# Attention with a mixture-of-experts tail: buffers for the bias groups, the place of the k, q and table loads, and the tiling of the reciprocals

## The chip, the cores and the metric

One NeuronCore of a Trainium2 chip runs the whole kernel. The metric is device time in microseconds (us). The kernel before takes 1065.97 us in the median of three runs (1064.12 to 1066.11).

## The reference, cut to what matters

Attention over 2 batches, 8 heads, 576 positions and 64 dimensions per head, with a position bias that a small network computes from the distance of two positions; two mixture-of-experts layers follow.

```python
scores = scale * np.matmul(q, k.transpose(0, 1, 3, 2))
psi_rel = np.log1p(np.abs(rel)); psi_i = np.log1p(np.maximum(pos[:, None], 1.0))
h = np.maximum((psi_rel / psi_i)[..., None] @ w1 + b1, 0.0)
bias = h @ w2                                   # one plane per head, the same for both batches
scores = scores + bias.transpose(2, 0, 1)[None]
attn = np.exp(scores - max); attn = attn / (sum + 1e-9)
x = attn @ v; x = moe(x); return moe2(x)
```

## The kernel before, in words

**Bias groups.** The 576 rows of the bias are computed in 36 groups of 16 rows, and eight groups make one 128-row chunk of the bias, `nb`. For a group g, `h_pieces` (L511) computes four hidden planes of 576 columns, each one instruction on a window of a table `win` of logarithms: for even groups VectorE (DVE) and ScalarE (ACT) do two each, for odd groups DVE does three and ACT one. `b_pieces` (L525) multiplies them on TensorE (PE) with the output weights into a PSUM bank pair, copies that, scaled by a row's factor, to an SBUF buffer `r` (the "out" of a group: for the first nine groups on DVE if g is even and on ACT if it is odd, afterwards on DVE), and a DMA spreads `r` over the partitions of `nb` (the "row" of a group, 288 KB). Hidden planes have two buffers (`hbs`), `r` has three (`rs2`), and the first nine groups take turns in three PSUM pairs, `pB`, `pT`, `sc`. `sc` is also the pair of the scores.

**Scores.** The first attention tile needs all eight rows of the first chunk. `s_pieces` (L628) multiplies q and k for one head into `sc`; one custom DVE instruction (in the trace `CUSTOM_DVE_ANT_0`) adds the bias from `nb` and finds the extreme; ACT takes the exponential. Transposes (`t_pieces`) and the product with v (`v_pieces`, column tiles of 128x64) follow. There are 9 tiles of 8 heads. `over` (L715) makes reciprocals of the sums and spreads them over partitions by four matmuls with 128x128 weights, twice a tile.

**Loads.** q and k arrive in float32 and are split in two float16 parts. For k (`load_k`, L565, four heads a load, two DMAs of 288 KB) DVE casts and subtracts. For q (`load_q`, L580) ACT casts and, for the first two loads, DVE subtracts. The staging buffers `stg` are two, and the loads take turns in them. k0 (heads 0 to 3 of batch 0), q0, the cast of the identity and k2 (heads 4 to 7) stand ahead of the bias groups in the program; the second part of the table, which only groups from 8 on read, is loaded behind the row of group 2 (`load_table`, ACT scales it). The dictionary `loads` (L620) says behind which group's row each other load is issued. All these DMAs are issued by SP, one queue.

**Order.** The program is recorded and then ordered by a planner (`Plan`, L47): every operation has an assumed cost, a due time counted back from the end and its data dependencies; an engine takes the ready operation that is due first. Marks (`plan.order`) add dependencies that data doesn't give. What the planner fixes is the order on each engine; on the chip each instruction then waits for its own inputs. One plan covers the bias, the attention and the start of the first expert layer. The work behind it is planned separately.

Of the kernel before, what the change touches and what calls it, by code (L numbers as in the profile page):

```python
# [10 lines left out]
F32 = mybir.dt.float32  # L11
# [3 lines left out]
ACTF = mybir.ActivationFunctionType  # L15
# [10 lines left out]
HS = 288  # L26
# [321 lines left out]
def attn_moe_moe_kernel(ctx: ExitStack, tc: tile.TileContext, a, out):  # L348
# [37 lines left out]
    def carve(t, *parts, off=0):  # L386

        out = []
        for shape, dtype in parts:
            out.append(at(t, off, shape, dtype))  # L390
            off += -(-int(np.prod(shape)) * mybir.dt.size(dtype) // 64) * 64
        return out
# [3 lines left out]
    def turn_of(ring):  # L396
        i = turns[id(ring)] = turns.get(id(ring), -1) + 1
        return ring[i % len(ring)]
# [15 lines left out]

    nbv = [at(t, 0, [H, S], F32) for t in nbr]
    hbs = carve(r_bias, *[([4, S], F32)] * 2)
    win, per_row = carve(r_bias, ([ROW0 + S], F32), ([144 + 36], F32), off=18432)
    shift, ipsi = per_row[:, 0:144], per_row[:, 144:]
    rs2 = carve(r_bias, *[([S], F32)] * 2, off=23744) + [at(r_w, 6144, [S], F32)]
# [8 lines left out]
    es2 = carve(r_e, *[([2 * S], F32)] * 3)  # L428
    ets = carve(r_e, *[([9, 128], F32)] * 2, off=13824)
    rbs, xts = (carve(t, *[([2, 128], F32)] * 2, off=o) for t, o in ((r_st, 8192), (r_e, 23040)))  # L430
    stg = [at(r_st, 0, [2, S], F32), at(r_w, 512, [2, S], F32)]
    wpk, sst = carve(r_w, ([2 + H], F32), ([4, H], F32))
    mns = [sml.tile([128, H], F32, name=f"mn{i}") for i in range(2)]
# [24 lines left out]
    pheads = psum_pool("pheads", 1, stack)  # L458
    sc, pT, pB = (pheads.tile([128, 1024], F32, name=n) for n in ("sc", "pT", "pB"))
    pO, pR = (pheads.tile([128, 512], F32, name=n) for n in ("pO", "pR"))  # L460
    pb0, pb = [pB, pT, sc], [pB]

    blk4 = const.tile([128, 4], F32, name="blk4")
    cst, ident16, ones, lg, P, pt, rs, cs, wgs, wg = carve(
# [26 lines left out]
    def warm(ps, n):  # L491
        with plan.together():
            for _ in range(n):
                pe.matmul(out=ps, lhsT=idle[:, 0:128], rhs=idle[:, 0:ps.shape[-1]], start=True, stop=True,
                          skip_group_check=True)

    warm(pO, 9)

    vec.tensor_scalar(shift, shift, b1, None, ALU.mult)
    vec.tensor_scalar(w2r, w2r, C_S, None, ALU.mult)  # L500
# [9 lines left out]

    def h_pieces(g):  # L511

        hb = hidden[g] = turn_of(hbs)

        def piece(u):
            m = ROW0 - rows_of[g][4 * u]
            x, by = win[:, m:m + S], shift[:, 4 * g + u:4 * g + u + 1]
            if u in BY_VECTOR[g % 2]:
                vec.tensor_scalar(hb[:, u], x, by, 0.0, ALU.add, ALU.max)
            else:  # L520
                act.activation(hb[:, u], x, ACTF.Relu, bias=by)

        return [lambda u=u: piece(u) for u in range(4)]

    def b_pieces(g):  # L525

        c, q = groups[g]
        r = turn_of(rs2)
        if q == 0:
            nbs[c] = turn_of(nbv)  # L530

        def piece():
            ps = turn_of(pb0 if g < EARLY else pb).rearrange("p (j n) -> p j n", j=2)[:, :, 0:HS]
            with plan.together():
                for jh in range(2):
                    for u in range(4):
                        pe.matmul(
                            out=ps[32 * u:32 * u + 32, jh], lhsT=sst, rhs=hidden[g][:, u, jh * HS:jh * HS + HS], start=True,
                            stop=True, tile_position=(0, 32 * u), skip_group_check=True,
                        )  # L540
            two = r.rearrange("p (j n) -> p j n", j=2)
            if g < EARLY and g % 2:
                act.activation(two, ps, ACTF.Copy, scale=ipsi[:, g:g + 1])
            else:
                vec.tensor_scalar(two, ps, ipsi[:, g:g + 1], None, ALU.mult)
            nb = nbs[c]
            with plan.order(mark=[("rows", g)]):
                if c < 4:
                    sp.dma_start(out=nb[q::8], in_=r)
                else:  # L550
                    for b in range(B):
                        for p in range(2):
                            sp.dma_start(out=nb[64 * b + q + 4 * p:64 * b + 64:8], in_=r[64 * p:64 * p + 64])
            for load, which in loads.get(g, ()):
                load(which, [("rows", g)])

        return [piece]
# [7 lines left out]
    def load_k(p, behind=()):  # L565

        (b, h), t = divmod(2 * p, H), turn_of(stg).rearrange("p i (j n) -> p (i j) n", j=2)
        for half in range(2):
            me = slice(64 * half, 64 * half + 64)
            load(t[me], a["kT"][me, 2 * p:2 * p + 4, HS * half:HS * half + HS], behind)  # L570
        hi, lo = (x[b][:, h:h + 4] for x in (kh, kl))
        vec.tensor_copy(hi, t)
        tt(vec, lo, t, hi, ALU.subtract)

    for b in range(B):
        for half in range(2):
# [3 lines left out]
    def load_q(t, behind=()):  # L580

        b0, n, c0, w = (t % 2, 1, 128 * (t // 2), 128) if t < 8 else (0, 2, 512, 64)
        x = turn_of(stg).rearrange("p i s -> p (i s)")[:, 0:1024].rearrange("p (h w) -> p h w", w=w)
        load(x, a["qT"][:, H * b0:H * b0 + H * n, c0:c0 + w], behind)
        for b in range(b0, b0 + n):
            xb = x[:, H * (b - b0):H * (b - b0) + H]
            hi = qh[:, 4 * b:4 * b + 4].rearrange("p i j s -> p (i j) s")[:, :, c0:c0 + w]
            act.activation(hi, xb, ACTF.Copy)
            for lo, h in [(qls[0], 0)] if b == 0 else [(qls[1], 0), (qls[2], 4)]:
                n_ = lo.shape[1]  # L590
                tt(vec if t < 2 else pool, lo[:, :, c0:c0 + w], xb[:, h:h + n_], hi[:, h:h + n_], ALU.subtract)

    def load_v(b, behind=()):

# [14 lines left out]
    def load_constants(i, behind=()):  # L609
# [2 lines left out]
        load(cst[:, j], a["cst"][:, j], behind)  # L612

    load_table(0)
    load_k(0)
    load_q(0)
    load_constants(0)
    vec.tensor_copy(ident16, ident)
    load_k(2)
    loads = {  # L620
        2: [(load_table, 1)], 7: [(load_v, 0)], 8: [(load_k, 4), (load_q, 1)], 9: [(load_k, 6)], 10: [(load_v, 1)],
        12: [(load_q, 2)], 13: [(load_q, 3), (load_constants, 1)], 18: [(load_q, 4)], 19: [(load_q, 5)],
        24: [(load_q, 8)], 27: [(load_q, 6)], 28: [(load_q, 7)],
    }
# [90 lines left out]
    def over(t, a_):  # L715

        s = state[t]
        (r, rs_), rb = turn_of(r4s), turn_of(rbs)
        vec.tensor_scalar(r, s["sm"][:, 4 * a_:4 * a_ + 4], 1e-9, 1.0 / C_X, ALU.add, ALU.mult)
        vec.reciprocal(r, r)  # L720
        rw = r.unsqueeze(2).to_broadcast([128, 4, D])
        eng = vec if t in ROW_TILES[-2:] else pool
        eng.tensor_copy(rs_[:, 0], rw)
        tt(eng, rs_[:, 1], rw, rs_[:, 0], ALU.subtract)
        ps = pR[:, 0:256].rearrange("p (k i) -> p k i", k=2)
        with plan.together():
            for k in range(2):
                for i in range(2):
                    pe.matmul(
                        out=ps[:, k], lhsT=rs_[:, i, 2 * k:2 * k + 2].rearrange("p h d -> p (h d)"),  # L730
                        rhs=ident16, start=(i == 0), stop=(i == 1), skip_group_check=True,
                    )
        act.activation(rb, ps, ACTF.Copy)
        s["r", a_] = rb

# [832 lines left out]
```

## Time and profile before

| | |
|---|---|
| median of 3 runs | 1065.97 us (1064.12 to 1066.11) |
| the profiled execution's own time | 1066.24 us |
| its span, first to last instruction | 1064.5 us |
| mean granted TensorE clock | 0.983 |
| PE busy | 94% of the span |
| DVE busy | 77% |
| ACT busy | 64% |

The shares are means over stages with different limits, so the page's totals don't say what bounds the start. For that the trace is asked stretch by stretch: the busy time of each engine in a window, then the instructions of an engine in order of time, where a bracket behind an instruction gives the idle time just before it and what ended it. Nearly all instructions carry line 159, the line of the planner's recorder, so they are told apart by the tiles that they write and read: `r_bias<-r_bias` is a hidden plane, `r_bias<-pB` (or `pT`, `sc`) an out, `nb<-r_bias` and `nb<-r_w` the rows, `r_k` k and `r_q` q.

### The profile page before, as it was taken

What the parts mean: (1) busy time and instruction counts of PE and PEld (TensorE: products, weight loads), DVE (VectorE), ACT (ScalarE), POOL (GpSimd) and SP (SyncE); (2) the same over time, 40 slices, a digit from 0 to 9 for tenths busy, and PEclk for the clock granted to TensorE, in tenths of its full rate; (3) what the DMA queues carried; (4) which work ended last, traced back from release to release, by engine and by line L of the source; (5) the groups of instructions that cost most, each with busy time, mean ns of one, the idle gap of its engine ahead of it and who ended that gap; (6) DMA issues with size and microseconds to landing.
All of it is one profiled execution on the core that took longest, in us unless ns stands there. A gap on an engine that the chain in (4) does not pass through costs nothing. (4 is left out here: it accounts for less than half of the span.)

```text
span 1064.5 us, 29649 instructions
## 1 busy us (share of the span) xinstructions
PE 1001.4 (94%) x12454; PEld 898.9 (84%) x12454; DVE 815.3 (77%) x1302; ACT 681.7 (64%) x1099; POOL 292.0 (27%) x249
## 2 busy tenths in 40 slices
PE   7799888999899999999999999999999999888996
PEld 3466556899899999999999999999999999656673
DVE  6898767576749779779779778787787887877982
ACT  5799888524356648548557557566576665667872
POOL 0034232005523223224133143132332210173220
PEclk9999999999899999999999999999999999899998
DMA  7953553003773375187077167257355023148693
GB/s 160 230 141 104 121 144 107 2 2 117 166 172 83 68 181 133 39 178 165 28 167 172 33 158 175 40 143 171 69 124 111 1 88 120 71 110 209 190 312 96
DMA packets 88869, 130.43 MB, mean 123 GB/s; under 512 B 19967, under 2 KB 51792, under 8 KB 88474
## 3 DMA queue, kind: packets, MB, share of 16 engines
q1 hardware_dynamic: 70826, 93.60, 30.9%
q0 software_dynamic: 17904, 34.88, 18.1%
q8 instruction: 99, 1.62, 0.6%
q14 instruction: 40, 0.33, 0.1%
HBM read 109.53 MB, written 5.29 MB: 108 GB/s over the span
## 5 line engine op out<-in xcount | busy, mean ns | idle before, releaser
L159 PEld LDWEIGHTS <-r_bias 128*128 128x128 f16 x4920 | 399.9, 98 | 8.5 <-issue 6.8
L159 PEld LDWEIGHTS <-r_v 128*128 128x128 f16 x2880 | 235.8, 98 | 7.0 <-issue 5.0
L159 PE MATMUL pb<-r_k,r_bias 128*128 128x192 f16 x2304 | 205.5, 247 | 0.7 <-ACT r_e L159 0.7
L159 POOL TENSOR_TENSOR r_q<-r_w,r_q 128x768 f16<-128x768 f32 x42 | 92.2, 2196 | 216.9 <-ACT r_q L159 211.1
L159 PE MATMUL pb<-nb,r_v 128*128 128x192 f16 x1260 | 151.2, 246 | 0.0
L159 PE MATMUL pb<-r_q,r_bias 128*128 128x192 f16 x1512 | 132.5, 246 | 0.0
L159 PE MATMUL pb<-nb,r_e 128*128 128x192 f16 x756 | 103.6, 246 | 0.0
L159 PEld LDWEIGHTS <-r_e 128*128 128x128 f16 (+2 forms) x1219 | 100.0, 98 | 2.0 <-issue 1.2
L159 PE MATMUL pb<-xa,r_v 128*128 128x192 f16 x1008 | 97.9, 246 | 0.0
L159 ACT ACTIVATE r_e<-pb 128x384 f32<-128x384 f32 (+1 forms) x96 | 48.2, 505 | 55.7 <-PE pb L159 55.2
L159 ACT ACTIVATE r_w<-pb 128x384 f32<-128x384 f32 x96 | 46.5, 488 | 57.9 <-PE pb L159 56.3
L159 POOL DMA_DIRECT2D r_st<-r_st x42 | 43.1, 1026 | 121.9 <-DMA r_st<-in_m1w 53.2
L159 POOL DMA_DIRECT2D r_e<-r_e x42 | 42.8, 1019 | 89.9 <-DMA r_e<-in_m1w 22.3
L159 ACT ACTIVATE r_e<-r_e,mn 128x576 f32<-128x576 f32 x72 | 56.2, 780 | 16.2 <-DVE mn L159 16.1
L159 DVE SCALAR_TENSOR_TENSOR r_bias<-r_st,r_bias 128x1024 f16<-128x1024 f32 (+1 forms) x45 | 51.3, 1156 | 18.1 <-ACT r_bias L159 17.6
L159 DVE CUSTOM_DVE_ANT_0 r_e<-sc,nb 128x576 f32<-128x576 f32 x72 | 54.1, 751 | 12.5 <-PE sc L159 12.2
L159 DVE TENSOR_TENSOR r_q<-r_w,r_q 128x384 f16<-128x384 f32 x42 | 61.0, 1451 | 0.0
L159 ACT ACTIVATE r_bias<-r_st 128x1024 f16<-128x1024 f32 (+1 forms) x45 | 43.6, 985 | 21.9 <-PE pb L159 17.8
L159 PEld LDWEIGHTS <-xa 128*128 128x128 f16 (+1 forms) x255 | 21.9, 104 | 40.1 <-issue 13.7
L159 ACT ACTIVATE r_q<-r_w 128x1152 f16<-128x1152 f32 (+1 forms) x46 | 52.9, 1150 | 3.1 <-DMA r_w<-in_qT 2.9
L159 ACT ACTIVATE r_e<-pT 128x512 f32<-128x512 f32 x72 | 46.5, 646 | 7.5 <-PE pT L159 7.3
L159 PEld LDWEIGHTS <-r_q 64*128 64x128 f16 (+2 forms) x560 | 26.5, 98 | 28.2 <-issue 25.4
(256 smaller groups left out, 1977.7 us busy)
## 6 DMA issues: line engine op xcount, KB each, us to landing
r_k<-in_m2w SPq DMA_DIRECT2D x48, 512.0 KB
r_st<-in_m2w SPq DMA_DIRECT2D x24, 512.0 KB
r_e<-in_m2w SPq DMA_DIRECT2D x24, 512.0 KB
r_st<-in_m1w SPq DMA_DIRECT2D x22, 512.0 KB
r_st<-in_m1w SPq DMA_DIRECT2D x42, 256.0 KB
r_e<-in_m1w SPq DMA_DIRECT2D x42, 256.0 KB
r_e<-in_m1w SPq DMA_DIRECT2D x14, 512.0 KB
r_st<-r_st POOLq DMA_DIRECT2D x14, 512.0 KB, 5.4
```

The costliest lines, as they stand in the source:

```text
L159: self.add(e, lambda: f(*a, **k), cost, dma, ins, outs, port, tiles)
```

## The change

The first eight groups get four buffers for hidden planes (two of them in the space of the second chunk of the bias, which is not yet in use) and nine for `r` (six of them in the space of later exponentials and transposes). Groups 6 to 8 leave `sc` out of their turn. The splits of k0 and q0 and the cast of the identity are not recorded ahead of the groups but behind the out of groups 2, 4 and 5, by a new mark; their DMAs stay at the start. The load of the second part of the table goes from behind row 2 to behind row 3, and the load and split of k2 from the start to behind row 6. The warm-up of TensorE has 13 matmuls instead of 9. `over` uses eight matmuls with 64 weight columns each, in the two column tiles that the product with v uses.

```diff
     hbs = carve(r_bias, *[([4, S], F32)] * 2)
+    hbs0 = hbs + carve(nbr[1], *[([4, S], F32)] * 2)
...
+    rs0 = rs2 + [x[:, S * i:S * i + S] for x in es2[2:] + [at(r_e, 13824 + 4608 * i, [2 * S], F32) for i in range(2)]
+                 for i in range(2)]
...
-    pb0, pb = [pB, pT, sc], [pB]
+    pb0, pb1, pb = [pB, pT, sc], [pB, pT], [pB]
...
-    warm(pO, 9)
+    warm(pO, 13)
...
-        hb = hidden[g] = turn_of(hbs)
+        hb = hidden[g] = turn_of(hbs0 if g < 8 else hbs)
...
-        r = turn_of(rs2)
+        r = turn_of(rs0 if g < 8 else rs2)
...
-            ps = turn_of(pb0 if g < EARLY else pb).rearrange("p (j n) -> p j n", j=2)[:, :, 0:HS]
+            ps = turn_of(pb0 if g < 6 else pb1 if g < EARLY else pb).rearrange("p (j n) -> p j n", j=2)[:, :, 0:HS]
...
-            if g < EARLY and g % 2:
-                act.activation(two, ps, ACTF.Copy, scale=ipsi[:, g:g + 1])
-            else:
-                vec.tensor_scalar(two, ps, ipsi[:, g:g + 1], None, ALU.mult)
+            with plan.order(mark=[("out", g)]):
+                if g < EARLY and g % 2:
+                    act.activation(two, ps, ACTF.Copy, scale=ipsi[:, g:g + 1])
+                else:
+                    vec.tensor_scalar(two, ps, ipsi[:, g:g + 1], None, ALU.mult)
...
-        vec.tensor_copy(hi, t)
-        tt(vec, lo, t, hi, ALU.subtract)
+
+        def split():
+            vec.tensor_copy(hi, t)
+            tt(vec, lo, t, hi, ALU.subtract)
+
+        return split if p == 0 else split()
...
     load_table(0)
-    load_k(0)
-    load_q(0)
+    splits = [load_k(0), load_q(0), lambda: vec.tensor_copy(ident16, ident)]
     load_constants(0)
-    vec.tensor_copy(ident16, ident)
-    load_k(2)
+
+    def split_first(i, behind):
+
+        with plan.order(behind=[("out", behind[0][1])]):
+            splits[i]()
+
     loads = {
-        2: [(load_table, 1)], 7: [(load_v, 0)], 8: [(load_k, 4), (load_q, 1)], 9: [(load_k, 6)], 10: [(load_v, 1)],
+        2: [(split_first, 0)], 3: [(load_table, 1)], 4: [(split_first, 1)], 5: [(split_first, 2)], 6: [(load_k, 2)], 7: [(load_v, 0)], 8: [(load_k, 4), (load_q, 1)], 9: [(load_k, 6)], 10: [(load_v, 1)],
...
-                    pe.matmul(
-                        out=ps[:, k], lhsT=rs_[:, i, 2 * k:2 * k + 2].rearrange("p h d -> p (h d)"),
-                        rhs=ident16, start=(i == 0), stop=(i == 1), skip_group_check=True,
-                    )
+                    for half in range(2):
+                        pe.matmul(
+                            out=ps[64 * half:64 * half + 64, k], lhsT=rs_[:, i, 2 * k + half], rhs=ident16, start=(i == 0),
+                            stop=(i == 1), tile_position=(0, 64 * half), skip_group_check=True,
+                        )
```

`load_q` is changed in the same way as `load_k`: for its first load it returns its split as a function.

## Rows read from the trace of the kernel before

**Rows 1.** Busy time by stretch (us): PE, PEld, DVE, ACT, POOL, clock, DMA share, GB/s.
```profile
5.66:31.45 25.79, 18.05 (x166) 7.94 (x167) 21.12 (x39) 16.98 (x25) 0.00 (x0) 1.00 0.79 175
31.45:60.00 28.55, 23.15 (x357) 15.56 (x358) 25.57 (x59) 22.54 (x45) 3.94 (x5) 0.94 1.06 244
60.00:110.00 50.00, 47.40 (x780) 31.94 (x780) 45.00 (x105) 48.46 (x104) 20.77 (x24) 1.00 0.41 105
...
205.00:1064.00 859.00, 826.19 (x9761) 780.98 (x9757) 656.90 (x940) 515.43 (x764) 243.18 (x181) 0.98 0.49 121
```

**Rows 2.** DVE in order of time, up to the first score: start us, us, what, idle before.
```profile
5.66 2.24 DVE L159 TENSOR_SCALAR r_bias<-r_bias 128x576 f32<-128x576 f32 x5
9.35 0.76 DVE L159 CAST r_k<-r_st 128x1152 f16<-128x1152 f32 x1 [1.45 <-DMA r_st<-in_kT]
10.88 0.23 DVE L159 CAST r_e<-r_e 128x128 f16<-128x128 f32 x1 [0.78 <-DMA r_e<-in_cst]
11.03 1.35 DVE L159 TENSOR_TENSOR r_k<-r_st,r_k 128x1152 f16<-128x1152 f32 x1
...
16.75 1.22 DVE L159 TENSOR_TENSOR r_e<-r_w,r_q 128x1024 f16<-128x1024 f32 x1
...
24.82 0.95 DVE L159 TENSOR_SCALAR r_bias<-r_bias 128x576 f32<-128x576 f32 x2 [2.03 <-ACT r_bias L159]
...
31.45 0.76 DVE L159 CUSTOM_DVE_ANT_0 r_e<-sc,nb 128x576 f32<-128x576 f32 x1 [0.18 <-DMA nb<-r_bias]
```

**Rows 3.** ACT in order of time, the same stretch.
```profile
10.68 1.06 ACT L159 ACTIVATE r_q<-r_w 128x1024 f16<-128x1024 f32 x1 [2.91 <-DMA r_w<-in_qT]
...
20.62 0.74 ACT L159 ACTIVATE r_bias<-pB,r_bias 128x576 f32<-128x576 f32 x1 [3.02 <-DMA nb<-r_bias]
...
24.14 0.65 ACT L159 ACTIVATE r_bias<-r_bias,r_w 128x424 f32<-128x424 f32 x1 [0.16 <-DMA r_bias<-in_xwin]
...
26.32 0.74 ACT L159 ACTIVATE r_bias<-pT,r_bias 128x576 f32<-128x576 f32 x1
```

**Rows 4.** Groups of instructions, 5.66 to 31.45 us: count, busy us, mean ns of one.
```profile
L159 ACT ACTIVATE r_bias<-r_bias 128x576 f32<-128x576 f32 x18 | 12.9, 767 | 2.6 <-DVE r_bias L159 1.5 <-PE pB L159 1.0
L159 DVE TENSOR_SCALAR r_bias<-r_bias 128x576 f32<-128x576 f32 x26 | 11.9, 516 | 2.0 <-ACT r_bias L159 2.0
...
L159 DVE TENSOR_SCALAR r_bias<-pB,r_bias 128x576 f32<-128x576 f32 x3 | 2.4, 814 | 0.2 <-DVE r_bias L159 0.2
```

**Rows 5.** PE in order of time: the warm-up, group 0, a late group.
```profile
1.33 4.02 PE L159 MATMUL pO<-xa 128*128 128x512 f16 x9 [1.33 <-POOL xa L159]
6.49 2.33 PE L159 MATMUL pB<-r_bias,r_w 128*32 128x288 f32 x13 [1.14 <-ACT r_bias L159]
...
27.78 1.22 PE L159 MATMUL pB<-r_bias,r_w 128*32 128x288 f32 x16 [0.29 <-ACT r_bias L159]
```

**Rows 6.** SP's queue in order of time: k2, rows 6 and 7, k4.
```profile
12.40 1.31 SPq L159 DMA_DIRECT2D r_st<-in_kT  x2
...
26.53 1.18 SPq L159 DMA_DIRECT2D nb<-r_bias  x2
...
31.18 1.26 SPq L159 DMA_DIRECT2D r_w<-in_kT  x2
```

**Rows 7.** DVE and PE in order of time: the cast of k4, its first use, batch 1.
```profile
40.88 0.76 DVE L159 CAST r_k<-r_w 128x1152 f16<-128x1152 f32 x1 [2.07 <-DMA r_w<-in_kT]
...
50.61 0.28 PE L159 MATMUL sc<-r_k,r_k 64*128 64x288 f16 x2
```

**Rows 8.** Busy time by stretch, columns as in rows 1: after the wait for k4.
```profile
44.00:48.00 4.00, 3.18 (x34) 2.89 (x33) 4.00 (x11) 3.33 (x7) 1.20 (x2) 0.57 0.97 190
```

**Rows 9.** Weight loads, 0 to 205 us: the reciprocals', then one of 64-column float16 loads.
```profile
L159 PEld LDWEIGHTS <-r_w 128*128 128x128 f16 x72 | 4.1, 97 | 2.5 <-issue 1.2 <-POOL r_w L159 0.5
...
L159 PEld LDWEIGHTS <-xa 128*64 128x64 f16 x8 | 0.3, 112 | 0.1
```

**Rows 10.** DVE in order of time, 108 to 121 us: a wait for a row.
```profile
116.53 0.82 DVE L159 TENSOR_SCALAR r_bias<-pB,r_bias 128x576 f32<-128x576 f32 x1 [3.61 <-DMA nb<-r_bias]
```

More of the change, by code (lines that the diff above doesn't have):

```diff
@@ L584, in load_q, with split @@
         load(x, a["qT"][:, H * b0:H * b0 + H * n, c0:c0 + w], behind)
[L585 to L591, printed above, removed]
+        def split():
+            for b in range(b0, b0 + n):
+                xb = x[:, H * (b - b0):H * (b - b0) + H]
+                hi = qh[:, 4 * b:4 * b + 4].rearrange("p i j s -> p (i j) s")[:, :, c0:c0 + w]
+                act.activation(hi, xb, ACTF.Copy)
+                for lo, h in [(qls[0], 0)] if b == 0 else [(qls[1], 0), (qls[2], 4)]:
+                    n_ = lo.shape[1]
+                    tt(vec if t < 2 else pool, lo[:, :, c0:c0 + w], xb[:, h:h + n_], hi[:, h:h + n_], ALU.subtract)
+        return split if t == 0 else split()
     def load_v(b, behind=()):
```

## The prediction

> **What bounds the kernel now.** I read the busy times by stretch first [rows 1]. From 205 us on PE is busy 826.19 of 859 us; that part is planned separately, the change doesn't touch it, and it can only begin earlier or later. From 60 to 110 us ACT is busy 48.46 of 50 us. The lead, from the first hidden plane at 5.66 us to the first score at 31.45 us, is bound by no engine: DVE is busy 21.12 of 25.79 us and ACT 16.98. From 31.45 to 60 us DVE is busy 25.57 of 28.55 us and the DMA engines have no pause (share 1.06).
>
> Next I read DVE and ACT in order of time through the lead, for what they wait for [rows 2, 3]. DVE stands 1.45 us for k0, 0.78 us for the identity and 2.03 us for the table's second part. ACT stands 2.91 us for q0 and 3.02 us at the out of group 3, because `r` has three buffers and that one is still being read by the DMA of row 0. ACT's waits lie on the chain: out 3 at 20.62 us, three planes, out 5, the table (0.65 us), two planes of group 8, and out 7 at 26.32 us, which ends at 27.06 us. SP issues rows 6 and 7 from 26.53 us [rows 6], and the first score starts at 31.45 us, 0.18 us after the wait for `nb` began. So 31.45 - 27.06 = 4.4 us pass from the last out to the first score, and everything later hangs on that score.
>
> **The change part by part.**
>
> *Buffers and moved splits.* I work out the earliest end of the lead from the unit prices [rows 4]: a plane takes 11.9/26 = 0.46 us on DVE and 12.9/18 = 0.72 us on ACT, an out 0.81 us, and 0.74 us on ACT [rows 3, 4]. Groups 0 to 7 need 4x2 + 4x3 = 20 planes and 4 outs on DVE, and 4x2 + 4x1 = 12 planes and 4 outs on ACT. ACT: 12x0.72 + 4x0.74 = 11.6 us, so 17.2 us on the clock of the trace; with q0's cast (1.06), the table (0.65) and two planes of group 8 in front, 20.4 us. DVE up to the last plane of group 7: 20x0.46 + 4x0.81 = 12.4 us, so 18.1 us; with k0's split (0.76 + 1.35), q0's (1.22) and the identity (0.23) in front [rows 2], 3.56 us more, 21.7 us; with two planes of group 8 too, 22.6 us. Then the matmuls of group 7 (1.22) [rows 5] and its out (0.74): 20.1 to 24.6 us. DVE's chain is the later. With the 4.4 us from out to score the first score falls at 24.5 to 29.0 us. I take the middle, 26.7 us: the new marks force k0's split only behind out 2 and q0's behind out 4, so they can lie in the shadow of row 7's transfer, but nothing says that the planner uses it. **First score earlier by 31.45 - 26.7 = 4.75 us**; ends 6.95 and 2.45.
>
> *k2.* Its load moves from 12.40 us, when the queue had no rows yet, to behind row 6, ahead of or behind row 7, v0 and k4. Its two DMAs take SP 1.31 us to issue [rows 6], which hides in their transfer: 2 x 288 KB = 0.59 MB at 244 GB/s [rows 1] is 2.4 us. If it is in front of row 7, row 7 and the first score are 2.4 us later; behind row 7 it costs nothing there. k2 also reuses k0's staging buffer, so it can't start before k0's split is done, which speaks for behind; I take 0, ends 0 and +2.4. Its split, 0.76 + 1.35 = 2.11 us on DVE, leaves the lead (my DVE sum above has it out already) and enters the first heads, where DVE has 28.55 - 25.57 = 2.98 us of pause. Those pauses are waits of their own and not all usable: I take half as paid, **+1.05 us**, ends 0 and 2.11. Queued behind it on DVE are the next scores' custom instructions, and behind those ACT's exponentials.
>
> On that queue the Trainium skill (DMA: Bandwidth & Descriptors, Queues, rings and completion order) says that each DMA engine takes descriptors in ring order; by it a k2 issued ahead of row 7 goes ahead of it on all engines, the +2.4 us end. The trace agrees as far as it goes: k4, issued at 31.18 us behind v0, was waited for until 40.88 us.
>
> *Other loads.* DMA work behind row 7 only moves forward with the lead. k4 landed at 40.88 us and is first used with batch 1's scores at 50.61 us [rows 7], so it has 9.7 us of slack in need; what it costs is the place the planner gave its cast. Cost 0, and in the next rival what it costs if the cover is gone. The table moves by one row; only group 8 reads it. 0.
>
> *Warm-up.* Four more matmuls at 4.02/9 = 0.45 us end it at 5.35 + 1.8 = 7.1 us instead of before 6.49 us, when group 0 started [rows 5]. Group 0 starts 0.6 us later at worst. In return the array doesn't fall idle: 13 instructions of group 0 took 2.33 us, where 16 later took 1.22 [rows 5], so up to 1.6 us is to be had. DVE has the planes of groups 1 to 3 to do meanwhile. 0; if that cover fails +0.6.
>
> *`sc` out of the turn of groups 6 to 8.* The first score waited for `nb`, not for `sc` [rows 2]. 0.
>
> *Reciprocals.* 18 times four 128-column loads, 72 in 4.1 us with 2.5 us of idle ahead of them, become 144 loads of 64 columns; the row nearest to these has 8 in 0.3 us [rows 9], so 144 take 5.4 us. From -2.5 (all idle gone, since the shape is then that of the product with v) to +1.3 us on PE. ACT is what fills 60 to 110 us [rows 1]; 0.
>
> The page TensorEngine Tiling (Array Packing) of the Trainium skill (Restrictions) speaks against this part: column tiles switch off the fast weight load. If each narrow load then cost as much as a wide one, PE would pay 4.1 us more; rows 9 have the narrow ones cheaper, and no run shows the two kinds of the same tile.
>
> *The new plan.* The whole order up to 205 us is planned anew. It can lose or gain a wait like DVE's 3.61 us for a row at 116.53 us [rows 10]. I take 0, ends -3.6 and +3.6.
>
> **Sum:** -4.75 + 1.05 = -3.7 us. The profiled run took 1066.24 us, 1.74 us more than its span, so 1062.5 us; the median of the runs shown is 0.27 us below the profiled one, so **1062.2 us**.
>
> **Rivals.**
>
> *All of it carries.* The splits lie in the shadow of row 7, and k2's split finds pauses: -6.95 us, 1059.0 us. For it: ACT is the limit from 60 us on and doesn't do k2's split. Against it: DVE is nearly as full (45.00 of 50 us).
>
> *k2 in front of row 7* eats it: the first score at 26.7 + 2.4 = 29.1 us, -2.35 us, and k2's split paid at 1.05 to 2.11: between -1.3 and -0.25 us, some 1065.2 us. For it: the DMA engines have no pause from 31.45 us on, and this adds 0.59 MB there. Also here, if the planner puts the splits back where the engines wait for the loads, so that the change does little of what it says.
>
> *Slower: DVE stands at a late k.* The planner puts a load's split where it believes the load has landed. At 40.88 us DVE stood 2.07 us at k4's cast; the scores behind it stood too, and after that PE's granted clock was 0.57 from 44 to 48 us [rows 7, 8], most of it at 1.2 instead of 2.4 GHz, which costs up to 0.43 x 4 = 1.7 us. A second stand of that kind at k2, with its split in full (2.11 us): 2.07 + 1.7 + 2.11 = 5.9 us. With k2 in front of row 7 as well the lead gains only 2.35 us: +3.5 us, 1069.5 us. It decides once the first score comes later than 31.45 - 5.9 = 25.6 us and DVE stands at k2. Against it: k2 isn't needed before the fifth head, so its split has the whole of four heads to land in.
>
> **How the numbers follow.** Forecast 0.5 (its own range 1060 to 1064.5), all carried 0.15, eaten 0.23, slower 0.12. What a measurement of this kernel can tell from no change is about 0.2%, 2.1 us: faster is below 1063.8, slower above 1068.1. Faster: most of the forecast (0.47) and the full carry, 0.62. Within: the rest of the forecast and the eaten case, 0.26. Slower: 0.12. The range leaves out the slower rival and the lower edge of the full carry: 1058.5 to 1067.0. It holds the new plan's 3.6 us on either side of the forecast.
>
> **What would show it.** Right: the waits for k0, q0, the identity and out 3 gone from DVE and ACT before 20 us; the first custom DVE instruction at 24 to 29 us; the start of the second part of the kernel some 4 us earlier. k2's place would show in SP's queue against row 7. Wrong: the first score no earlier than 29.1 us; or earlier, but with new waits for `r_st<-in_kT` on DVE and a clock below 1 in the heads behind it; or a later wait for a row that is longer than 3.61 us.

## The result and the profile after

The changed kernel takes **1072.64 us** (median; 1067.73 to 1076.57) where the kernel before, on the same chip, takes 1065.36 us (1061.88 to 1066.35): ratio **1.0088, 95% interval 1.0073 to 1.0103**. It is slower, by 0.88%; the forecast was 1062.2 us. The profiled execution of after took 1074.15 us, its span is 1072.4 us against 1064.5 us for the kernel before, so 7.9 us are to be found.

The busy times by stretch, columns as in [rows 1]:

```profile
5.66:31.45 25.79, 18.11 (x185) 8.36 (x186) 21.21 (x43) 18.28 (x29) 0.00 (x0) 0.81 0.85 197
31.45:60.00 28.55, 21.99 (x320) 14.46 (x316) 22.19 (x47) 19.24 (x38) 3.45 (x5) 0.87 0.79 169
60.00:110.00 50.00, 45.99 (x726) 29.39 (x723) 45.65 (x101) 45.21 (x93) 19.04 (x21) 0.97 0.45 118
...
205.00:1072.00 867.00, 835.38 (x9933) 790.06 (x9927) 663.01 (x957) 520.86 (x779) 242.28 (x181) 0.98 0.48 120
```

The loss lies ahead of 205 us. DVE and ACT each do over 3 us less between 31.45 and 60 us than before, at a lower clock, and ACT, which filled 48.46 of the 50 us behind that, is busy for 45.21. To see where, I follow the start of each head's score (the custom DVE instruction, 72 of them; the first is number 0). Times in us, read off DVE in order of time, each kernel in one profiled execution:

| score | before | after | after - before |
|---|---|---|---|
| 0 | 31.45 | 26.72 | -4.73 |
| 2 | 35.26 | 31.40 | -3.86 |
| 5 | 44.01 | 37.28 | -6.73 |
| 6 | 45.90 | 45.66 | -0.24 |
| 13 | 63.92 | 64.22 | +0.30 |
| 18 | 73.65 | 80.47 | +6.82 |
| 50 | 146.84 | 154.75 | +7.91 |
| 58 | 169.88 | 182.27 | +12.39 |
| 71 | 199.51 | 209.64 | +10.13 |

Three steps: the lead wins 4.7 us, scores 5 to 6 lose 6.5 us, scores 13 to 18 lose another 6.5 us. Behind that the distance swings between 5.5 and 12.4 us, and the part behind the attention ends 7.9 us late.

**The lead.** DVE in order of time; the columns are those of [rows 2]:

```profile
17.04 0.76 DVE L159 CAST r_k<-r_st 128x1152 f16<-128x1152 f32 x1
17.70 1.23 DVE L159 TENSOR_TENSOR r_e<-r_w,r_q 128x1024 f16<-128x1024 f32 x1
18.84 1.36 DVE L159 TENSOR_TENSOR r_k<-r_st,r_k 128x1152 f16<-128x1152 f32 x1
22.50 2.24 DVE L159 TENSOR_SCALAR r_bias<-r_bias 128x576 f32<-128x576 f32 x5 [2.30 <-ACT r_bias L159]
24.65 0.22 DVE L159 CAST r_e<-r_e 128x128 f16<-128x128 f32 x1
...
26.72 0.76 DVE L159 CUSTOM_DVE_ANT_0 r_e<-sc,nb 128x576 f32<-128x576 f32 x1 [1.75 <-PE pB L159]
```

The waits for k0, q0 and the identity are gone: their splits stand at 17 to 25 us, behind their marks. DVE stands 2.30 us for ACT instead. ACT's stand at out 3 is gone too, and one for the table has come in its place. ACT in order of time:

```profile
16.90 0.74 ACT L159 ACTIVATE r_e<-sc,r_bias 128x576 f32<-128x576 f32 x1 [0.94 <-PE sc L159]
21.82 0.65 ACT L159 ACTIVATE r_bias<-r_bias,r_w 128x424 f32<-128x424 f32 x1 [4.17 <-DMA r_bias<-in_xwin]
22.37 0.72 ACT L159 ACTIVATE r_e<-pT,r_bias 128x576 f32<-128x576 f32 x1
```

The table's second part is now loaded behind row 3, SP issues it at 14.87 us, and the planner put its use (for group 8) ahead of out 7. The 4.17 us at the table replace the 3.02 us at out 3 in [rows 3]. Out 7 ends at 23.09 us, 3.6 us before the first score.

**The first loss.** DVE, then PE, in order of time:

```profile
37.28 0.75 DVE L159 CUSTOM_DVE_ANT_0 r_e<-sc,nb 128x576 f32<-128x576 f32 x1
...
44.25 0.76 DVE L159 CAST r_k<-r_w 128x1152 f16<-128x1152 f32 x1 [5.19 <-DMA r_w<-in_kT]
44.93 0.81 DVE L159 TENSOR_SCALAR r_bias<-pB,r_bias 128x576 f32<-128x576 f32 x1
45.66 0.75 DVE L159 CUSTOM_DVE_ANT_0 r_e<-sc,nb 128x576 f32<-128x576 f32 x1
```

```profile
46.47 0.66 PE L159 MATMUL sc<-r_k,r_q 64*128 64x288 f16 x4 [5.43 <-DVE mn L159]
```

DVE reaches the cast of k4 at 39 us and stands there for 5.19 us, where it stood 2.07 us before [rows 7]. Score 6 is behind it in DVE's queue and PE behind score 6. In the same stretch ACT stands 3.44 us for q1, which it did not before:

```profile
42.48 1.06 ACT L159 ACTIVATE r_q<-r_st 128x1024 f16<-128x1024 f32 x1 [3.44 <-DMA r_st<-in_qT]
```

SP's queue shows why k4 is no earlier although the lead is shorter. In order: rows 5 to 7, k2, v0, row 8, row 9, the first half of k4, q1, the second half of k4.

```profile
17.16 6.50 SPq L159 DMA_DIRECT2D nb<-r_e  x3
23.75 1.32 SPq L159 DMA_DIRECT2D r_st<-in_kT  x2
25.12 0.59 SPq L159 DMA_DIRECT2D r_v<-in_vfull  x1
25.76 1.25 SPq L159 DMA_DIRECT2D r_v<-in_vtail  x2
28.25 0.57 SPq L159 DMA_DIRECT2D nb<-r_bias  x1
31.46 0.58 SPq L159 DMA_DIRECT2D nb<-r_bias  x1
32.09 0.64 SPq L159 DMA_DIRECT2D r_w<-in_kT  x1
33.89 0.38 SPq L159 DMA_DIRECT2D r_st<-in_qT  x1
34.32 0.63 SPq L159 DMA_DIRECT2D r_w<-in_kT  x1
```

k4's halves are issued at 32.09 and 34.32 us, no earlier than before (31.18 us, both, [rows 6]). Its load is recorded behind row 8. Group 8 reads the table's second part, which came late, so row 8 goes out at 28.25 us, hardly earlier than before (28.54 us). The planner has also put row 9 in front of k4, and row 9 waits for out 9, which stands behind k2's cast on DVE: it goes out at 31.46 us. Between k4's halves stands q1, which is loaded into k2's staging buffer and so waits for k2's split (until 33.86 us). DVE, for both:

```profile
29.77 0.76 DVE L159 CAST r_k<-r_st 128x1152 f16<-128x1152 f32 x1 [0.45 <-DMA r_st<-in_kT]
30.61 0.82 DVE L159 TENSOR_SCALAR r_bias<-pB,r_bias 128x576 f32<-128x576 f32 x1
...
32.51 1.35 DVE L159 TENSOR_TENSOR r_k<-r_st,r_k 128x1152 f16<-128x1152 f32 x1
```

And k2's 0.59 MB, which before went out at 12.40 us in the lead, now lie in the queue ahead of all of them, from 23.75 us. The stretches around the stand, columns as in [rows 1]:

```profile
20.00:30.00 10.00, 5.69 (x42) 2.04 (x41) 5.50 (x15) 6.22 (x10) 0.00 (x0) 0.58 0.76 176
30.00:41.00 11.00, 10.49 (x162) 6.97 (x155) 8.98 (x20) 7.78 (x17) 1.21 (x2) 0.92 1.11 215
41.00:46.00 5.00, 0.03 (x2) 0.05 (x1) 1.75 (x3) 2.48 (x4) 0.00 (x0) 0.95 1.05 272
46.00:52.00 6.00, 5.53 (x54) 3.25 (x55) 4.83 (x10) 4.25 (x8) 0.00 (x0) 0.50 0.67 167
```

The queue moves 215 GB/s while k4 waits its turn; the planner counts with 360 (line 146), so it can place the cast where the load hasn't landed yet. Behind PE's 5 idle us the granted clock is 0.50, all of it at the lower level (1.2 instead of 2.4 GHz), for 6 us. The lead had such a stretch already, 0.58 from 20 to 30 us, while ACT waited for the table. (The page DMA: Bandwidth & Descriptors of the Trainium skill, Queues, rings and completion order, has the descriptors of a ring taken in order. The trace fits that: q1, issued between k4's halves, is waited for until 42.48 us, and k4 until 44.25 us, 9.9 us after its second half was issued.)

**The second loss**, scores 13 to 18, has no single wait: DVE stands for less than 1 us at any instruction there. The hidden planes on DVE, 54 to 80 us, as a group (count, busy us, mean ns of one):

```profile
L159 DVE TENSOR_SCALAR r_bias<-r_bias 128x576 f32<-128x576 f32 x16 | 10.7, 701 | 0.0
```

In the kernel before the same group has 18 planes at 570 ns:

```profile
L159 DVE TENSOR_SCALAR r_bias<-r_bias 128x576 f32<-128x576 f32 x18 | 9.7, 570 | 0.0
```

What differs is what runs beside them. Planes that no TENSOR_TENSOR of POOL overlaps take 505 ns before and 503 ns after (means). A plane that runs beside POOL's subtractions for q takes up to 1.72 us in after, and 0.98 us at most before. POOL, then DVE, in order of time, in after:

```profile
65.44 2.50 POOL L159 TENSOR_TENSOR r_k<-r_w,r_q 128x512 f16<-128x512 f32 x2 [0.27 <-ACT r_q L159]
68.39 2.30 POOL L159 TENSOR_TENSOR r_e<-r_st,r_q 128x1024 f16<-128x1024 f32 x1 [0.44 <-ACT r_q L159]
69.28 1.72 DVE L159 TENSOR_SCALAR r_bias<-r_bias 128x576 f32<-128x576 f32 x1
```

What the planes take beyond that is 16 x 0.20 = 3.1 us in after and 18 x 0.065 = 1.2 us before: some 2 us of the 6.5 (an estimate from these means). The trace doesn't say where the rest goes. So the experiments have two questions: is the stand at k4 the cause of the first loss, and does the second come from a part of the change or from the new order as such?

### The profile page after: what moved, and what is told of

It is laid out like the page before. It is cut to its first block, busy times and chain, and to the rows that moved or that the text cites. A ratio compares the mean times of both kernels' runs of the same rounds, so it can differ in the third digit from the quotient of the medians.

```text
span 1072.4 us, 29784 instructions
## 1 busy us (share of the span) xinstructions
PE 1006.3 (94%) x12530; PEld 901.8 (84%) x12530; DVE 820.2 (76%) x1302; ACT 682.8 (64%) x1099; POOL 290.4 (27%) x249
```

## The experiments

Each ratio is to the kernel before, timed on the same chip. From chip to chip its median lies between 1059.53 and 1065.36 us, so where an expectation gives a range in us, the ratio is what counts. Starts of scores come from one profiled execution of each kernel.

### Does k4's stand take the lead's gain?

**k2_early**: after, with k2's load behind row 2 instead of row 6.

```
-        2: [(split_first, 0)], ... 5: [(split_first, 2)], 6: [(load_k, 2)], ...
+        2: [(split_first, 0), (load_k, 2)], ... 5: [(split_first, 2)], ...
```

> The changed kernel, but k2 is loaded behind row 2 instead of behind row 6; nothing else differs. Theory (queue): k4's cast stood 5.19 us on DVE because k2's 0.59 MB went into the queue among the loads that k4 waits for. Then k4 lands about 2.4 us earlier, the wait at its cast falls to 3 us or less, and the time to 1067 to 1070. Rival (work): DVE and ACT simply have more to do in the first heads; then the wait may shrink but the time stays at 1071 to 1074. Rival (clock): the half clock from 21 to 31 us is what costs; then the time stays too as long as that stretch stays.

**table_early**: after, with the table's second part loaded at the start.

```
+    load_table(1)
...
-        ... 3: [(load_table, 1)], ...
```

> The changed kernel, but the second part of the table is loaded at the start instead of behind row 3. ACT stood 4.17 us for it in the lead with the out of group 7 queued behind. The first score should come 2 to 4 us earlier, at 23 to 25 us, and the half clock before it should go. Theory (queue): the gain is eaten, because k4 lands when the queue lets it; its wait grows to 6 to 9 us and the time stays at 1070 to 1074. Rival (lead): the lead carries through to the end; then 1068 to 1070.

**hold_k4**: after, with k4's split planned only behind score 6, and k6's load recorded behind it.

```
...
+        with plan.order(behind=[("score", 0, 6)]):
+            splits[3]()
+        load_k(6, [("rows", 9)])
...
```

> The changed kernel, but k4's split may not stand on DVE ahead of the seventh head's score (it is first needed at the ninth head); k6's load, which takes turns with it in the staging buffer, is recorded behind it. No load is issued earlier. Theory (place): the 5.19 us at k4's cast are lost because heads 7 and 8 are queued behind a cast that they don't need; then the wait falls under 2 us and the time to 1066 to 1069. Rival (queue alone): the wait for k4 only comes two heads later, just as long; time 1071 to 1074.

**buffers_only**: the kernel before with `hbs0`, `rs0` and `pb1` alone; splits, loads, warm-up and reciprocals as before.

> The kernel before with nothing but the buffers: four for hidden planes, nine for r, sc out of the turn of groups 6 to 8. Splits, loads, warm-up and reciprocals are those of before; k2 is loaded behind k0's split as before. If the buffers give the earlier first score (about 27 us or earlier) and the moved loads take it back, this is faster than before: 1061 to 1064. If the buffers alone bring the loss (heads too early for the loads), it is 1068 or more.

| kernel | median us | ratio | interval | score 0 | score 14 |
|---|---|---|---|---|---|
| k2_early | 1067.71 | 1.0017 | 0.9996 to 1.0038 | 25.70 | 65.19 |
| table_early | 1066.68 | 1.0005 | 0.9985 to 1.0026 | 24.91 | 64.40 |
| hold_k4 | 1069.04 | 1.0030 | 1.0006 to 1.0053 | 27.37 | 64.88 |
| buffers_only | 1066.06 | 1.0017 | 0.9999 to 1.0035 | 26.09 | 65.04 |

All four start the scores 4 to 6.5 us early. The buffers alone give the lead's gain; the marks aren't needed for it, since with the buffers the planner by itself puts k0's cast at 16.68 us instead of 9.35. None has a stand at k4 like that of after (buffers_only 2.28 us, the others none), scores 5 to 6 lose at most 1.4 us instead of 6.5, and each is faster than after. So the first loss is the stand. In k2_early k2 still goes out behind row 7, 2.8 us earlier than in after, and both halves of k4 from 28.28 us, ahead of row 9 and of q1. In table_early row 8 goes out at 26.43 us and both halves of k4 from 30.27 us, ahead of q1. The lower clock in the lead is not what costs: table_early has 0.54 and 0.50 from 21 to 31 us and yet the earliest first score.

But none turns the gain into time; all have lost it by score 14 (before: 65.33 us; after: 68.61). That was not expected of table_early, which came out under both of its ranges without the longer wait for k4, and buffers_only lies between its two. In k2_early and table_early the stand has moved on to k6. DVE in order of time, in k2_early and then in table_early:

```profile
53.60 0.76 DVE L159 CAST r_k<-r_w 128x1152 f16<-128x1152 f32 x1 [3.44 <-DMA r_w<-in_kT]
```

```profile
53.77 0.76 DVE L159 CAST r_k<-r_w 128x1152 f16<-128x1152 f32 x1 [5.35 <-DMA r_w<-in_kT]
```

There are two staging buffers, so k6's load waits for k4's split, and v1 comes in front of it on SP in both. In the other two the stand is at a q, on ACT. hold_k4, where DVE waits for ACT's cast of q1 (ACT itself stood 3.29 us for the load):

```profile
43.36 0.69 DVE L159 TENSOR_TENSOR r_k<-r_st,r_q 128x512 f16<-128x512 f32 x1 [2.11 <-ACT r_q L159]
```

buffers_only, ACT, at the place where it loses 3.4 us between scores 13 and 14:

```profile
65.29 1.06 ACT L159 ACTIVATE r_q<-r_st 128x1024 f16<-128x1024 f32 x1 [2.38 <-DMA r_st<-in_qT]
```

So a cure for one load leaves the scores at the next one. What a shorter lead uncovers is the chain of loads as a whole.

### The planner's beliefs

**jit_a** and **jit_b**: after, with the delay that the planner adds to a transfer at 660 and 640 ns instead of 650. The work is the same, the order another: in jit_a k4's cast stands one instruction later on DVE, and ACT, POOL and SP keep after's order up to 205 us.

```
-    REACH, DMA_REACH, DMA_ISSUE, DMA_DELAY, OWN, GRAIN = 200.0, 900.0, 500.0, 650.0, 130.0, 64
+    REACH, DMA_REACH, DMA_ISSUE, DMA_DELAY, OWN, GRAIN = 200.0, 900.0, 500.0, 660.0, 130.0, 64
```

> The changed kernel with the planner's assumed DMA delay at 660 instead of 650 ns: the program is the same, the order differs in few places (k4's cast stands one instruction later on DVE). Theory (loads): the wait for k4 is again about 5 us and the time 1071 to 1075. Rival (chance of the plan): the changed kernel merely drew a bad order and any other order is some 4 us better; then 1066 to 1069.

> The same with 640 ns: the order differs in many places, and k4's cast stands one head earlier on DVE. Theory (loads): the wait for k4 is 6 to 8 us, time 1071 to 1076. Rival (chance of the plan): 1066 to 1069.

**rate220**: after, with the planner counting 220 instead of 360 GB/s for transfers up to the end of the attention.

```
+    RATE = 220.0
...
-            dma = min(out.nbytes(), k["in_"].nbytes()) / (150.0 if "accum_op" in k else 360.0) + 10
+            dma = min(out.nbytes(), k["in_"].nbytes()) / (150.0 if "accum_op" in k else self.RATE) + 10
...
+    plan.RATE = 360.0
```

> The changed kernel, but the planner assumes 220 instead of 360 GB/s for the loads up to the end of the attention (about what the profile shows when the queue is full), so that it places casts where loads really land. Theory (place): the waits for k4 and k6 on DVE fall under 2 us together, and of the earlier first score (about 27 us) some stays: 1063 to 1067. Rival (queue alone): heads are held up elsewhere by as much, 1070 to 1074.

**rate_before**: the kernel before with that lower rate alone. **rate_table**: rate220 and table_early together.

> The kernel before, with the planner told 220 instead of 360 GB/s for transfers up to the end of the attention; no buffers, no marks, no tiles. Theory (the planner's belief in transfers that are too early is what costs, and the change only laid it bare): waits for k gone here too, but the lead still ends at about 31 us for want of buffers, ratio 0.998 to 1.001. Rival (the lower rate alone gives rate220's gain): 0.995 to 0.998.

> The kernel after with both cures: 220 instead of 360 GB/s in the planner, and the table's second part loaded at the start instead of behind row 3. Theory (lead and staging chain both cured): first score at 24.5 to 26 us, no DVE wait for a k over 1.5 us, heads 5 to 8 us ahead of before up to head 30, ratio 0.994 to 0.998. Rival (the gain meets the stage that ACT fills and goes there, whatever the lead does): 0.998 to 1.001.

| kernel | median us | ratio | interval | longest DVE wait for k4 or k6 |
|---|---|---|---|---|
| jit_a | 1071.53 | 1.0105 | 1.0075 to 1.0136 | 6.11 |
| jit_b | 1067.80 | 1.0085 | 1.0056 to 1.0115 | 2.10 |
| rate220 | 1057.44 | 0.9985 | 0.9961 to 1.0008 | none |
| rate_before | 1070.32 | 1.0078 | 1.0048 to 1.0109 | 0.26 |
| rate_table | 1060.83 | 0.9982 | 0.9960 to 1.0003 | none |

rate220's profiled execution keeps the lead's gain: the waits for k4 and k6 are gone, k6 is issued ahead of v1, and score 36 is still 5.15 us ahead of before, where after is 7.78 us behind. Its time isn't clear of the kernel before, though. And a belief nearer to the trace is no cure by itself. rate_before, with hardly a wait for k left, starts its scores 1.73 us late and comes out about as slow as after, outside both of its ranges: without the added buffers the lower rate only makes another order, and a worse one. Nor does rate_table's earlier score 0 (24.55 us) add anything to rate220 that shows; its ratio is in the rival's range.

jit_a does what its theory said, and keeps the stand at k4. jit_b doesn't: the stand was expected to grow to 6 to 8 us and is 2.10, and the kernel is slower than before all the same. ACT stands 4.80 us for q1 there. The scores of its profiled execution, the fastest of five, are ahead of before's up to score 42 and level at the last; one execution doesn't show where the time goes.

### The tiles, or their plan?

**over_only**: the kernel before with the column-tiled reciprocals alone. **over_old**: after, with the reciprocals of before.

```
-                    pe.matmul(
-                        out=ps[:, k], lhsT=rs_[:, i, 2 * k:2 * k + 2].rearrange("p h d -> p (h d)"),
...
+                    for half in range(2):
+                        pe.matmul(
+                            out=ps[64 * half:64 * half + 64, k], lhsT=rs_[:, i, 2 * k + half], rhs=ident16, start=(i == 0),
```

> The kernel before with the reciprocals' matmuls in column tiles and nothing else. Forecast said 0 (ends -2.5 and +1.3 us). Theory: the matmul group stays at about 0.4 us and the time within 2 us of before, 1063.5 to 1067.5. Rival: the tiles are what the changed kernel lost, 1068 or more.

> The kernel after with the reciprocals of the kernel before (128-column loads); buffers, marks and loads stay. Theory (k4's late cast eats the lead's gain, and the plan that the tiling brings loses the other 6 us in heads 13 to 18): k4's wait of 4 to 5 us stays, head 10 within 1 us of before, heads 13 to 18 without the loss, ratio 1.001 to 1.005. Rival (the second loss comes from the late k4 too, through the bias groups that stand behind it): ratio 1.007 to 1.010, heads 13 to 18 again 6 us back.

over_only: 1066.72 us, ratio 1.0056 (1.0033 to 1.0080), slower than its theory allows: on this chip before takes 1059.53 us. over_old: 1067.27 us, 1.0044 (1.0024 to 1.0064), so after loses half of its slowness with the wide loads. Up to some 54 us DVE and ACT have after's order in it. over_old still stands at k4:

```profile
42.76 0.76 DVE L159 CAST r_k<-r_w 128x1152 f16<-128x1152 f32 x1 [4.18 <-DMA r_w<-in_kT]
```

and is level with before at score 10 (55.98 against 56.14 us), but at score 18 it is 1.69 us behind, where after is 6.82. From score 13 to 18 it loses 3.67 us and after 6.52, so what goes with the tiles, or with the order that they bring, is less than half of the second loss; theory and rival each had it all or nothing. The rest isn't the tiles': buffers_only, which has none, loses 4.66 us there, and k2_early, hold_k4 and table_early, which have them but no long stand at k4, lose 0.8 to 1.8. That the late k4 carries on into these scores is thus not excluded. The planner counts a tiled group at another cost and as a switch of tiles, so every order changes with it.

**tiles_alone**: over_only, with the planner told the old cost, so that every engine has the order of the kernel before.

```
+            if e == "t" and "pR" in out.tensor.name and "tile_position" in k:
+                tiles, cost = None, 0.0 if any(k["tile_position"]) else cost
```

> The kernel before with the column-tiled reciprocals alone, and the planner told that the eight narrow matmuls cost what the four wide ones did and are no tiles of their own, so that every engine has the order of the kernel before. Theory (the tiles are free, and the reciprocals' part changes the time only by the new plan that they bring): ratio 0.999 to 1.001, first score within 0.3 us of before, the pR groups 0.40 us each, the weight loads 144 in 4 to 5 us. Rival (the narrow loads and the tile switches themselves cost): over_only's ratio again, 1.004 to 1.008, with the heads behind each pR group falling back by 0.1 to 0.3 us.

1065.23 us, ratio 1.0022 (0.9998 to 1.0047): undecided. Its scores stay within 0.81 us of before's from 0 to 36 and end 0.42 us late (199.93 us), which speaks for free tiles; the interval doesn't exclude the rival.

**rate_old**: rate220 with the reciprocals of before. **rate_old_again**: the same kernel, timed again; **rate_tiles**: rate_old's order on every engine, with the tiles in it, by the same edit as tiles_alone.

> rate220 with the reciprocals of the kernel before. Theory (the tiles cost by their plan alone, so in a plan that is good with them taking them out makes one more new plan and brings no gain): 0.998 to 1.006. Rival (the tiles cost by themselves about 5 us in any plan): 0.993 to 0.996.

> rate_old once more, to see whether it beats the kernel before. Theory (buffers, late splits and a plan that fits, without the tiles, are faster): ratio 0.993 to 0.998. Rival (0.9953 was a draw of that chip): 0.998 to 1.001.

> rate_old's order on every engine, with the column-tiled reciprocals in it (planned at the cost of the wide ones), beside rate_old_again on the same chip. Theory (the tiles are free, only their plan costs): within 0.0015 of rate_old_again's ratio. Rival (they cost by themselves, as tiles_alone's 1.0022 would have it): 0.002 to 0.005 above it, and the heads behind the reciprocals fall back step by step.

rate_old: 1058.70 us, 0.9953 (0.9928 to 0.9979), which is in the rival's range, tiles that cost by themselves. rate_old_again: 1055.88 us, **0.9933 (0.9910 to 0.9956)**. rate_tiles, on the same chip: 1056.71 us, **0.9933 (0.9916 to 0.9950)**, and both profiled spans are 1057.4 us. Up to 205 us every engine has the same order in both. So in one order, on one chip, the tiles cost nothing that can be measured; by the two intervals that holds to within 0.3%, which leaves of the rival's 0.002 to 0.005 only the lower edge. rate_old's step from rate220 (0.9985) lies within the intervals of the two. The weight loads of the reciprocals up to 205 us, in rate_old_again and then in rate_tiles:

```profile
L160 PEld LDWEIGHTS <-r_w 128*128 128x128 f16 x72 | 4.3, 100 | 4.0 <-issue 1.7 <-POOL r_w L160 1.6
```

```profile
L162 PEld LDWEIGHTS <-r_w 128*64 128x64 f16 x144 | 4.8, 111 | 4.5 <-POOL r_w L162 2.1 <-issue 1.7
```

So over_only's 0.56% and the step from after to over_old are most likely the order's; in those orders the tiles were not tested apart. Both of these kernels beat the kernel before. And rate_tiles executes the same instructions as after, engine by engine; only what the planner was told differs, and with it the order. The same work is 0.88% slower than before in one order and 0.67% faster in the other, some 16 us apart.

### How much does a new order move the time?

**before_d600**, **before_d640**, **before_d700**: the kernel before with the planner's delay at 600, 640 and 700 ns, the edit of jit_a. They have none of the change's parts.

> The kernel before with one constant of the planner changed (the delay that it adds to a transfer, 600 instead of 650 ns), so that the same work is put in another order from the lead on. Theory (before's order is a lucky one among its neighbours, and any part that makes the plan anew costs up to 8 us by that alone): ratio 1.002 to 1.008. Rival (the plan's place has nothing to do with it; the change's own loads and tiles cost): ratio within 0.998 to 1.002.

> As before_d600, with 640 ns; the order differs from the kernel before only from about the thirtieth head on. Theory (a lucky order): 1.002 to 1.006. Rival: within 0.998 to 1.002.

> As before_d600, with 700 ns; the order differs from the kernel before only from about the thirtieth head on. Theory (a lucky order): 1.002 to 1.006. Rival: within 0.998 to 1.002.

| kernel | median us | ratio | interval |
|---|---|---|---|
| before_d600 | 1065.82 | 1.0033 | 1.0013 to 1.0053 |
| before_d640 | 1072.55 | 1.0107 | 1.0066 to 1.0148 |
| before_d700 | 1068.35 | 1.0051 | 1.0023 to 1.0078 |

All three are slower than before, by 3.5, 11.4 and 5.4 us of its 1062.65, the middle one beyond what was expected. The order of the kernel before is better than these neighbours, and an edit that makes it anew gives that up. Starts of the scores, us, read off DVE:

| score | before | after | over_old | rate_old_again | rate_tiles | before_d600 | before_d640 |
|---|---|---|---|---|---|---|---|
| 0 | 31.45 | 26.72 | 26.30 | 25.99 | 25.52 | 31.21 | 31.52 |
| 6 | 45.90 | 45.66 | 44.16 | 38.24 | 38.60 | 49.81 | 46.00 |
| 18 | 73.65 | 80.47 | 75.34 | 67.34 | 68.55 | 79.27 | 73.90 |
| 36 | 112.07 | 119.85 | 112.22 | 106.98 | 108.33 | 121.18 | 112.29 |
| 71 | 199.51 | 209.64 | 202.56 | 194.67 | 193.62 | 203.61 | 202.61 |

before_d600 is 5.6 us behind at score 18 with nothing but another order, and it has after's stand with none of the change's loads:

```profile
44.68 0.76 DVE L159 CAST r_k<-r_w 128x1152 f16<-128x1152 f32 x1 [4.74 <-DMA r_w<-in_kT]
```

ACT stands 5.96 us for q1 beside it. before_d640 has before's order on DVE up to 146 us and is only 3.1 us behind at the last score; where the rest of its 11.4 us goes isn't shown. before_d700 has that order up to 128 us and still starts score 18 at 75.42 us, 1.77 us late, so a difference of under 2 us between two executions says nothing about an order. rate_old_again keeps what the lead wins to the last score. Its stretches, columns as in [rows 1]:

```profile
5.66:31.45 25.79, 18.86 (x222) 9.29 (x221) 24.24 (x49) 20.46 (x34) 0.00 (x0) 0.93 0.96 211
31.45:60.00 28.55, 23.98 (x386) 16.17 (x387) 28.20 (x63) 24.57 (x49) 7.29 (x9) 1.00 1.03 226
60.00:110.00 50.00, 46.76 (x774) 31.88 (x768) 42.16 (x102) 48.46 (x102) 18.04 (x24) 1.00 0.43 115
```

DVE is busy for 28.20 of 28.55 us behind the lead, where after has 22.19: no stand of over 0.35 us at a k, and no fall of the clock there.

## Why the prediction was wrong, step by step

*Buffers and moved splits*: right that the buffers end the lead earlier, by the forecast amount; that it is 26.72 us against 26.7 is luck. I took DVE's chain for the later one and 4.4 us from the last out to the score. In after ACT's chain is the later, with 4.17 us at the table that I had not seen, and 3.6 us follow it. table_early, without that wait, has 24.91 us, still between the ends of 24.5 and 29.0.

*k2*: right for the lead. It went behind row 7 and cost the lead nothing. By score 2, with its cast done, 0.87 us were gone (-4.73 to -3.86, a stand of 0.45 us in it), forecast 1.05; by score 5 they were back (-6.73). What I left out is the queue behind it: its cast holds up row 9 and its split q1, and both stand ahead of k4 on SP.

*Other loads*: **the step that failed first.** I costed them at 0, since k4 "has 9.7 us of slack in need; what it costs is the place the planner gave its cast". The need didn't matter. The place did: with DVE 7 us earlier and k4 no earlier, its stand grew from 2.07 to 5.19 us, and scores 5 to 6 lost 6.49 us, nearly the whole gain. I wrote that work behind row 7 "only moves forward with the lead". k4 didn't: on SP row 8 stands in front of it, which waited for the table, whose move I had put at 0 ("only group 8 reads it"), and then row 9 and q1, which waited for k2's split. In table_early and in k2_early, which each put k4's second half out 3 to 5 us earlier, the stand at k4 is gone. Behind it stands a queue that gives 215 GB/s in after and gave 244 before, which a shorter lead doesn't make any faster.

*Reciprocals*: right. In one order, rate_tiles against rate_old_again, they cost nothing that can be measured. The rule that I cited from the Trainium skill (TensorEngine Tiling (Array Packing), Restrictions: column tiles switch off the fast weight load) fits the mean of one load, 111 ns for 64 columns against 100 for 128, but the 4.1 us that I worked out from it don't appear: the busy time of the loads grows by 0.5 us, beside matmuls. I had read the narrow loads as the cheaper ones; [rows 9] says otherwise, since its 0.3 and 4.1 us count overlapping loads once, and the means of one are 112 against 97 ns.

*The new plan*: **the second step that failed**, a term mis-sized. I gave it 0 with ends of 3.6 us, from one wait. Four orders of the kernel before with no part of the change in them cost, by their ratios, +3.5, +5.4, +8.3 (rate_before, 0.0078 of 1062.5) and +11.4 us, and rate_tiles, with the work of after, is some 16 us faster than after. Within after the step to over_old, 1.0088 to 1.0044, is some 4.7 us, most likely of the order that the tiles brought. The forecast was -3.7 us and the ratio says +9.4, a miss of 13 us; k4's stand (6.5 us) and this step (4.7 us) are most of that, but they aren't independent, since each edit that cures the stand makes the order anew too.

*Warm-up* and *`sc` out of the turn* had no experiment of their own. After the longer warm-up group 0 starts at 6.36 us, not later than before (6.49), and 13 of its matmuls take 1.59 us instead of 2.33 [rows 5]:

```profile
6.36 1.59 PE L159 MATMUL pB<-r_bias,r_w 128*32 128x288 f32 x13 [0.49 <-ACT r_bias L159]
```

Of the rivals, *Slower: DVE stands at a late k* was the right kind: a stand at a cast, then the clock down, on the side of 1069.5 us. It named k2; it was k4. I had put its chance at 0.12 because the argument against it looked at when k is needed, not at where the cast stands in DVE's queue.

What stays open is what after's 6.5 us in scores 13 to 18 are made of: some 2 us go with the planes that run beside POOL, which was read and not isolated, and whether the rest is the order's alone or a consequence of the late loads isn't shown. Nor is it shown how much of rate_old_again's and rate_tiles' gain is the shorter lead and how much the draw of the order.

## What to carry to other kernels

A lead that gets shorter is worth only what the next stage can take, and here that stage's limit was a queue of loads, with their casts planned in the middle of the compute: look at what the engine will stand at when it arrives early, not at when the data is needed. Where a planner orders everything, a small edit is also a new draw of the order; change the planner's constants without the edit first, to see how far a draw moves the time, and test an edit's parts in a fixed order. A tuned order is part of the kernel: here the same change came out 0.88% slower in its first order and 0.67% faster in another.

## What the runs showed that was not expected

A load of 64 columns takes as long as one of 128 (111 against 100 ns, means of 144 and 72), and the time of the kernel doesn't show it. A hidden plane on DVE takes 503 ns by itself and up to 1.72 us beside POOL's subtractions. PE's idle 5.43 us at k4 left it at the lower clock level for the 6 us from 46 to 52 us, granted clock 0.50, while in the kernel before, behind a stand of 2.07 us, it was 0.57 over 4 us [rows 8].
